# The order of work up to the first gate, written out anew, in a fused attention and expert kernel

## The chip, the cores and the metric

The kernel runs on one core of a Trainium2 chip. The metric is the device time of one execution in microseconds (us), lower is better. The profiler records one execution; all times inside it count from the start of its span.

## What is computed

```python
# attention with a decay, per batch (4), head (8); 576 tokens, 64 wide
scores = q @ k.T / 8 + (cum[:, None] - cum[None, :])    # cum = cumsum(log(clip(f, 1e-4, 1)))
attn = softmax(where(causal, scores, -1e9))
x = (attn @ v)            # heads side by side: (2304, 512)
# four experts, all used, weighted by p = domain_probs / sum
out = sum_e p[:, e] * (relu(x @ w1[e]) @ w2[e])          # w1: 512x1024, w2: 1024x512
```

## The kernel before

Attention is cut into jobs: a batch, a pair of heads and a part of the tokens (`half` 0: the first 256, `half` 1: the other 320). The output tokens are cut into nine chunks of 256. An expert's hidden units are cut into tiles of 128, and one weight tile holds the w1 columns (its columns 0 to 511) and the w2 rows (512 to 1023) of one such tile. A `Step` (L767) is one chunk against two weight tiles: `l1` gives the two tiles of hidden units, `gate` applies relu, `l2` multiplies by w2. Precision is kept by splitting an operand x into a rounded part (h) and the rest (l); a product is then three matmuls, h·h, h·l and l·h. A weight tile's rounded half (512 columns) is written by ScalarE (`w_hi`, L750), its rest by VectorE for even tiles of 2 to 14 and by GpSimd for the others (`w_lo`, L755). Even and odd tiles are the first and second of a step's two.

The work up to the first gate has an order of its own. The first four jobs (class `First`, L602; batch 0, first 256 tokens, two heads each, so heads 0 to 7) take plain fp32 products, all other jobs split ones. A head goes through: scores (`qk_pe`, L610), masked minimum (`qk_min`, L392, VectorE), exponential (`qk_exp`, L407, ScalarE), three transposes (`tr_pe`, L623), their copy out of PSUM (`tr_out`: ScalarE L634 for a pair's first head, VectorE L636 for its second), and the product with v (`av_pe`, L643). Per job, `recip` (L423, L426, L428: a tiny VectorE pair and a GpSimd copy) makes the reciprocal sums, `spread_out` transposes them (L451) and copies them out (L654, ScalarE), `scaled` multiplies (L658, VectorE, twice per job) and `fin` splits the result into `xh` and `xl`, on GpSimd (L669, L670) for jobs 0 to 2 and on ScalarE and VectorE (L672, L673) for job 3. After all four, step 0's `l1` can be finished; the hidden dimension of x is cut into four 128s, and block k comes from job k.

What sets the order: `startup` (L1083) runs in `tc.manual_schedule()`, so each engine keeps the order in which `startup` writes its instructions. Everything later is placed by a planner, which may also slip later instructions into a queue's gaps. `decays` (L143) makes the log decay rows: scans along the tokens (L115) of rows 0 and 1, and of all 32 rows, whose first 256 values then go by three small DMAs (L184) into row 64 of the other jobs' operands, so that one product adds scores and decay. `later_decays` (L193) scans the rest, splits it on ScalarE and VectorE (L197, L198), writes it to DRAM (L200), from where later jobs read it (L296), and issues the loads that follow, `w_load(3)` among them. All DMAs are issued from SP's queue. `W_HI` and `W_LO` (L33, L34) say after which head which half of weight tiles 0 to 3 is split.

Of the kernel before, what the change touches and what calls it, by code (L numbers as in the profile page):

```python
# [8 lines left out]
F32 = mybir.dt.float32  # L9
F32R = mybir.dt.float32r  # L10
AF = mybir.ActivationFunctionType
# [6 lines left out]
CH = 256  # L18
# [11 lines left out]
W_DVE = tuple(range(2, 16, 2))  # L30
LAST = (5, 6, 7, 8)
AHEAD = 10
W_HI = {2: ((0, 0),), 3: ((0, 512),), 4: ((1, 0),), 6: ((1, 512),), 7: ((2, 0), (2, 512)), 8: ((3, 0), (3, 512))}  # L33
W_LO = {**W_HI, 6: (), 7: ((1, 512),), 8: ((2, 0), (2, 512), (3, 0), (3, 512))}  # L34
JOBS = ((0, 0), (1, 0), (2, 0), (3, 0), (0, 1), (1, 1), (2, 1), (3, 1))


# [32 lines left out]
def fused(ctx: ExitStack, tc: tile.TileContext, qk, v, f, probs, w, out):  # L70
# [66 lines left out]
            )  # L137

    idle_ps = []
    wslot = {}  # L140
    vb = []

    def decays():  # L143
        for n in range(3, 9):
            x = xh_p.tile([128, NPR, CH], F32R, tag=("xl", "xh")[n % 2], name=f"wr{n}")
            wslot[n] = x.rearrange("p k n -> p (k n)").bitcast(F32)
        j = jobs[0]
        nc.sync.dma_start(out=row, in_=f[:2, :CH].rearrange("(o h) n -> o h n", o=1))
        nc.sync.dma_start(out=fr, in_=f)
        first_raw(0, (0,))  # L150
        first_raw(0, (1,))
        first_raw(1)
        first_raw(2)
        first_v(0)
        nc.vector.memset(ones, 1.0)
        nc.scalar.activation(out=warm, in_=ones[: B * H, :1], func=AF.Ln)
        nc.gpsimd.memset(jobs[0].kq[64:65, :, :CH], 8.0)
# [24 lines left out]
        scan(ncum[:, :CH], fr[:, :CH])  # L182
        for i in jobs[1:NPR]:
            nc.sync.dma_start(  # L184
                out=i.kq[64:65, :, CH:], in_=ncum[2 * i.pr : 2 * i.pr + 2, :CH]
            )
        first_raw(3)
        w_load(0)
        first_v(2)
        w_load(1)  # L190
        w_load(2)

    def later_decays():  # L193
        hi = xf_p.tile([128, 1024], F32R, tag="xf", name="nc_hi")[: B * H, :S]
        lo = scr2[: B * H, :S].bitcast(F32R)
        scan(ncum[:, CH:], fr[:, CH:], ncum[:, CH - 1 : CH])
        nc.scalar.activation(out=hi, in_=ncum, func=AF.Copy)  # L197
        nc.vector.tensor_tensor(out=lo, in0=ncum, in1=hi.bitcast(F32), op=ALU.subtract)  # L198
        for n, x in enumerate((hi, lo)):
            nc.sync.dma_start(out=ncd[:, n], in_=x.bitcast(F32))  # L200
        jobs[NPR].load()
        vb.append(acc_p.tile([128, 1024], F32, tag="acc", name="vb"))
# [30 lines left out]
            j.vs = slots[4][:, 256 * j.pr : 256 * j.pr + 256]  # L233

    def first_v(n):
        for j in jobs[n : n + 2]:
            nc.sync.dma_start(
                out=j.vs.rearrange("p (t h d) -> p t h d", t=2, h=2), in_=v[0, j.pr, :, :2]
            )

    def first_raw(n, heads_=(0, 1)):
        j = jobs[n]
# [359 lines left out]
    class First(Job):  # L602
# [24 lines left out]
                )  # L627
            self.tp[hh] = ps

        def tr_out(self, hh):  # L630
            n = 2 * self.pr + hh
            pt = self.pt[hh] = pt0[n % 2][:, 384 * (n // 2 % 3) : 384 * (n // 2 % 3) + 384]
            if hh == 0:
                nc.scalar.activation(out=pt, in_=self.tp[hh][:, :384], func=AF.Copy)  # L634
            else:
                nc.vector.tensor_copy(out=pt, in_=self.tp[hh][:, :384])  # L636

        def av_pe(self, hh):
            if hh == 0:
                self.o = ps_2.tile([128, 512], F32, tag="l2", name=f"o{self.nm}")  # L640
                self.xs = x_p.tile([128, 320], F32, tag="xs", name=f"xs{self.nm}")
            for jt, (a, z) in enumerate(((0, 256), (256, 384))):
# [10 lines left out]
            self.rc = x_p.tile([128, 320], F32, tag="tmp", name=f"rc{self.nm}")  # L653
            nc.scalar.activation(out=self.rc[:, :CH], in_=self.r[:, :CH], func=AF.Copy)  # L654

        def scaled(self, hh):
            a = slice(64 * hh, 64 * hh + 64)
            nc.vector.tensor_tensor(  # L658
                out=self.xs[a, :CH],
                in0=self.o[a, CH * hh : CH * hh + CH],  # L660
                in1=self.rc[a, :CH],
                op=ALU.mult,
            )

        def fin(self):
# [101 lines left out]
    class Step:  # L767
# [3 lines left out]
            self.nm = f"{s}_{g}_{c}_{ps}"  # L771

        def l1(self, q):
            if q == 0:
                self.l1p = ps_1.tile([128, 2, CH], F32, tag="l1", name=f"l1_{self.nm}")
            fi, kk = divmod(q, 2)
            th, tl = xh[self.c], xl[self.c]
            n = self.w0 + fi
            for k in (2 * kk, 2 * kk + 1):
                a = wh[n][:, k * 128 : (k + 1) * 128]  # L780
                z = wl[n][:, k * 128 : (k + 1) * 128]
                for m, (lhsT, rhs) in enumerate(((a, th), (a, tl), (z, th))):
                    nc.tensor.matmul(  # L783
                        out=self.l1p[:, fi, :],
                        lhsT=lhsT,
                        rhs=rhs[:, k, :],
                        start=(k == 0 and m == 0),
                        stop=(k == 3 and m == 2),
                    )

        def gate(self):
            self.gh = g_p.tile([128, 2, CH], F32R, tag="gh", name=f"gh{self.nm}")
            self.gl = g_p.tile([128, 2, CH], F32R, tag="gl", name=f"gl{self.nm}")
            nc.scalar.activation(out=self.gh, in_=self.l1p, func=AF.Relu)
            nc.vector.scalar_tensor_tensor(
                out=self.gl,
                in0=self.l1p,
                scalar=0.0,
                in1=self.gh.bitcast(F32),
                op0=ALU.max,  # L800
                op1=ALU.subtract,
            )

        def l2(self, q):
            tt, fi = divmod(q, 2)
# [276 lines left out]

    def startup():  # L1083

        def at(h):
            return heads[h] if 0 <= h < FIRST else (None, None)

        def scores(h):
            j, hh = at(h)
            if j:  # L1090
                j.begin(hh)
                j.qk_pe(hh, j.its)

        def mins(h):
            j, hh = at(h)
            if j:
                for t in j.its:
                    j.qk_min(hh, t)

        def exps(h):  # L1100
            j, hh = at(h)
            if j:
                for t in j.its:
                    j.qk_exp(hh, t)

        def close(j):
            for x in range(2):
                j.scaled(x)
            j.fin()

        first_slots()
        decays()
        scores(0)
        mins(0)
        exps(0)
        scores(1)
        mins(1)
        idle(256, 1)
        for s in range(FIRST + 1):
            (j, hh), (i, ii) = at(s), at(s - 1)  # L1120
            old = heads[s - 3][0] if s in (3, 5, 7) else None
            if s:
                scores(s + 2)
            if j:
                j.tr_pe(hh)
            if s == 0:
                scores(s + 2)
            exps(s + 1)
            if j:
                j.tr_out(hh)  # L1130
                if hh == 1:
                    j.recip()
            if s == FIRST:
                i.spread_out()
            if i:
                i.av_pe(ii)
            if old:
                old.spread_out()
            mins(s + 2)
            if old:  # L1140
                close(old)
            if s == FIRST:
                close(i)
            for n, a in W_HI.get(s, ()):
                w_hi(n, a, a + 512)
            for n, a in W_LO.get(s, ()):
                w_lo(n, a)
            if s == 1:
                later_decays()
# [113 lines left out]
```

## Time and profile before

| | |
|---|---|
| median of 3 runs | 977.52 us (975.76 to 978.43) |
| the profiled execution | 975.0 us, its span 973.2 us |
| TensorE busy in the span | 960.6 us, 99% |
| VectorE, ScalarE, GpSimd busy | 70%, 48%, 53% |
| granted TensorE clock, mean | 1.00 |
| bytes moved by DMA | 85.89 MB, 88 GB/s over the span |

The views are: the page's busy times; a table of stretches (windows); the chain of work that ended last, in order of time; and the timeline of one engine, where a row gives start, duration, engine, line, operation, output and inputs, and the count of instructions merged into it. In square brackets stands the idle time before the row, with what ended it.

### The profile page before, as it was taken

How to read it: one execution, taken by the hardware profiler on the slowest of the kernel's cores; microseconds unless marked ns; L12 is line 12 of the kernel's file. 1: busy time of each engine (PE TensorE's matmuls, PEld its weight loads, DVE VectorE, ACT ScalarE, POOL GpSimd, SP SyncE). 2: the span in 40 equal slices, each digit the busy share in tenths (PEclk: the TensorE clock that was granted, in tenths of full speed). 3: DMA queues.
4: the chain of work that ended last, by engine and by line, in shares of the span. 5: the costliest groups of instructions: out<-in, count | busy, mean ns of one | idle time of the engine just before them, and what ended most of it. 6: DMA issues, size and time to landing. Idle time of an engine off the chain costs nothing.

```text
span 973.2 us, 15567 instructions
## 1 busy us (share of the span) xinstructions
PE 960.6 (99%) x5638; PEld 843.7 (87%) x5638; DVE 676.4 (70%) x1413; ACT 467.2 (48%) x979; POOL 513.6 (53%) x511
## 2 busy tenths in 40 slices
PE   8999999999999999999999999999999999999998
PEld 6898999899899999998999998988788888888886
DVE  6877777877877676778769656357766666566665
ACT  7776664646656455556455544334323232233220
POOL 4988763502306547548457565778654444555410
PEclk9999999999999999999999999999999999999999
DMA  7765431322312312313313030421211112111002
GB/s 257 254 205 169 140 92 42 110 84 95 128 53 89 103 52 96 97 52 117 96 57 134 2 109 22 130 90 63 87 44 43 44 44 73 58 44 43 23 1 87
DMA packets 29822, 85.89 MB, mean 88 GB/s; under 512 B 3160, under 2 KB 5264, under 8 KB 29744
## 3 DMA queue, kind: packets, MB, share of 16 engines
q1 hardware_dynamic: 29744, 84.89, 26.8%
q8 instruction: 45, 0.74, 0.3%
q14 instruction: 33, 0.27, 0.1%
HBM read 80.00 MB, written 4.87 MB: 87 GB/s over the span
## 4 chain that ended last, share of the span: by engine, by line
PE 83%; POOL 5%; DVE 5%; issue 3%; DMA 2%; ACT 1%; SPq 0%; POOLq 0%; DVEq 0%; ACTq 0%
PE l L783 19%; PE l L813 19%; PE y L1011 17%; PE m L953 13%; PE s L378 5%; PE t L479 5%; PE o L529 5%; POOL bwl L933 2%; DMA wr<-in_w 2%; POOL wt L910 1%; POOL wl L755 1%; DVE v L313 1%; DVE kl L334 1%; POOL rx L895 1%; DVE rl L897 1%
## 5 line engine op out<-in xcount | busy, mean ns | idle before, releaser
L783 PE MATMUL l<-xl,wh 128*128 128x256 f32 x640 | 180.8, 283 | 0.3 <-DVE xl L673 0.3
L783 PE MATMUL l<-xh,wh 128*128 128x256 f32 x640 | 180.9, 283 | 0.2 <-ACT xh L672 0.2
L783 PE MATMUL l<-xh,wl 128*128 128x256 f32 x640 | 180.6, 283 | 0.0
L755 POOL TENSOR_TENSOR wl<-wr,wh 128x512 fp32r<-128x512 f32 x114 | 151.9, 1358 | 30.5 <-ACT wh L750 19.2
L835 DVE SCALAR_TENSOR_TENSOR acc<-y,prob,acc 128x512 f32<-128x512 f32 x120 | 88.3, 747 | 68.5 <-PE y L1011 68.5
L442 POOL TENSOR_SCALAR p<-p,rs 128x384 f32<-128x384 f32 (+2 forms) x72 | 107.8, 1513 | 50.1 <-DVE rs L438 46.8
L813 PE MATMUL l<-wh,gh 128*128 128x512 f32 x320 | 127.2, 397 | 0.8 <-DVE acc L835 0.8
L813 PE MATMUL l<-wl,gh 128*128 128x512 f32 x320 | 126.7, 396 | 0.0
L813 PE MATMUL l<-wh,gl 128*128 128x512 f32 x320 | 125.0, 394 | 0.0
L407 ACT ACTIVATE p<-p,nm 128x576 f32<-128x576 f32 (+2 forms) x160 | 95.6, 598 | 58.4 <-DVE nm L392 57.1
L783 PEld LDWEIGHTS l<-xl,wh 128*128 128x128 f32 x640 | 120.5, 188 | 3.3 <-DVE xl L673 0.5
L783 PEld LDWEIGHTS l<-xh,wh 128*128 128x128 f32 x640 | 120.4, 188 | 3.4 <-ACT xh L672 0.4
L933 POOL TENSOR_TENSOR bwl<-wr,bwh 128x256 fp32r<-128x256 f32 (+1 forms) x80 | 78.5, 1008 | 80.0 <-ACT bwh L930 80.0
L783 PEld LDWEIGHTS l<-xh,wl 128*128 128x128 f32 x640 | 120.4, 188 | 0.2
L392 DVE CUSTOM_DVE_ANT_0 p<-s,mask 128x288 f32<-128x288 f32 (+2 forms) x160 | 74.8, 478 | 57.6 <-PE s L378 52.4
L326 POOL CAST q<-raw 64x320 fp32r<-64x320 f32 (+1 forms) x56 | 27.3, 488 | 145.7 <-PE s L378 131.8
L1011 PE MATMUL y<-bwh,hh 128*128 128x512 f32 x256 | 101.2, 395 | 0.8 <-DVE acc L835 0.8
L1011 PE MATMUL y<-bwl,hh 128*128 128x512 f32 x256 | 101.1, 395 | 0.0
L1011 PE MATMUL y<-bwh,hl 128*128 128x512 f32 x256 | 100.4, 395 | 0.0
L953 PE MATMUL m<-rl,bwh 128*128 128x512 f32 x224 | 87.5, 390 | 0.0
L953 PE MATMUL m<-rh,bwh 128*128 128x512 f32 x224 | 87.4, 390 | 0.0
L953 PE MATMUL m<-rh,bwl 128*128 128x512 f32 x224 | 87.0, 392 | 0.0
(121 smaller groups left out, 2097.4 us busy)
## 6 DMA issues: line engine op xcount, KB each, us to landing
wr<-in_w SPq DMA_DIRECT2D x96, 512.0 KB
raw<-in_qk SPq DMA_DIRECT2D x16, 896.0 KB
raw<-in_qk SPq DMA_DIRECT2D x12, 512.0 KB
vr<-in_v SPq DMA_DIRECT2D x16, 320.0 KB
out<-acc SPq DMA_DIRECT2D x16, 256.0 KB
vr<-in_v SPq DMA_DIRECT2D x8, 128.0 KB
first<-in_qk SPq DMA_DIRECT2D x3, 256.0 KB
first<-in_v SPq DMA_DIRECT2D x4, 128.0 KB
```

The lines of the kernel that those rows point to most:

```text
L378: nc.tensor.matmul(out=ps[:, at : at + z - a], lhsT=lhsT, rhs=rhs, start=(m == 0), stop=(m == 1),)
L392: nc.vector.tensor_tensor_reduce(out=pt[:, a:z], in0=ps, in1=mask[:, m0 + a : m0 + z], scale=-0.125, scalar=BIG if n == 0 else nm[:, col : ...
L407: return nc.scalar.activation(out=pt[:, :w_], in_=pt[:, :w_], func=AF.Exp, scale=-1.0, bias=self.nmax[hh][:, c : c + 1], accum_out=self.ss ...
L442: eng.tensor_scalar(out=x, in0=x, scalar1=rs[:, i : i + 1], scalar2=None, op0=ALU.mult)
L479: nc.tensor.transpose(ps[:, at : at + 128], self.p[hh, it][:, TOK0[jt] : TOK0[jt] + 128], ident)
L755: eng.tensor_tensor(out=wl[n][:, a:z], in0=wraw[n][:, a:z], in1=wh[n][:, a:z].bitcast(F32), op=ALU.subtract)
L783: nc.tensor.matmul(out=self.l1p[:, fi, :], lhsT=lhsT, rhs=rhs[:, k, :], start=(k == 0 and m == 0), stop=(k == 3 and m == 2),)
L813: nc.tensor.matmul(out=l2[tt], lhsT=lhsT, rhs=rhs, start=(self.ps == 0 and fi == 0 and m == 0), stop=(self.ps == 1 and fi == 1 and m == 2),)
L835: nc.vector.scalar_tensor_tensor(out=acc[c][:, tt, :], in0=ps, scalar=sc, in1=acc[c][:, tt, :], op0=ALU.mult, op1=ALU.add,)
L933: nc.gpsimd.tensor_tensor(out=lo[:, a:z], in0=x[:, a:z], in1=hi[:, a:z].bitcast(F32), op=ALU.subtract)
L953: nc.tensor.matmul(out=ps, lhsT=lhsT[:, o], rhs=rhs[:, k, :], start=(k == 0 and i == 0), stop=(k == 1 and i == 2),)
L1011: nc.tensor.matmul(out=ps, lhsT=lhsT, rhs=rhs, start=(fi == 0 and m == 0), stop=(fi == 1 and m == 2),)
```

## The change

Six edits, all before or in step 0. (1) `decays`: clamps and logs go first for all three inputs, then the scans, the 32-row one second; only job 0's v is loaded ahead of the decay rows, job 1's after them; w tile 0 comes before job 3's q and k; two of GpSimd's row fills go to VectorE. (2) `later_decays` is cut in two: the scan of the rest stands right after head 0's transposes, its split is on GpSimd; the DMAs follow after head 2's minimum. (3) A head's product with v takes only that head's 64 columns of v, so that the two heads of a job fill 64 partitions each of the same 256 columns, and `scaled` is one VectorE operation. (4) `startup` is written out line by line. (5) Step 0's first products go pair by pair: block k of both weight tiles, then block k+1, in two PSUM tiles, with two gates of half the width. (6) Of the weight tiles 0 to 3, the w1 halves are split first, the w2 halves later.

```diff
@@ decays
         first_raw(1)
+        first_v(0)
         first_raw(2)
-        first_v(0)
...
-        for i in jobs[1:NPR]:
-            nc.gpsimd.memset(i.kq[64:65, :, :CH], 8.0)
+        for i, eng in zip(jobs[1:NPR], (nc.vector, nc.vector, nc.gpsimd)):
+            eng.memset(i.kq[64:65, :, :CH], 8.0)
...
-        for h in range(2):
-            clamp(row[:, h])
-            log(row[:, h])
+        rows = (row[:, 0], row[:, 1], fr)
+        for x in rows:
+            clamp(x)
+        for x in rows:
+            log(x)
+        nc.scalar.activation(out=warm, in_=ones[: B * H, :1], func=AF.Exp)
         scan(j.kq[64:65, 0, CH:], row[:, 0])
-        clamp(fr)
-        log(fr)
-        nc.scalar.activation(out=warm, in_=ones[: B * H, :1], func=AF.Exp)
+        scan(ncum[:, :CH], fr[:, :CH])
         scan(j.kq[64:65, 1, CH:], row[:, 1])
-        scan(ncum[:, :CH], fr[:, :CH])
         for i in jobs[1:NPR]:
             nc.sync.dma_start(
                 out=i.kq[64:65, :, CH:], in_=ncum[2 * i.pr : 2 * i.pr + 2, :CH]
             )
+        first_v(1)
+        w_load(0)
         first_raw(3)
-        w_load(0)
         first_v(2)
+        first_v(3)
         w_load(1)
         w_load(2)
-    def later_decays():
+    def far_decays():
...
-        nc.scalar.activation(out=hi, in_=ncum, func=AF.Copy)
-        nc.vector.tensor_tensor(out=lo, in0=ncum, in1=hi.bitcast(F32), op=ALU.subtract)
-        for n, x in enumerate((hi, lo)):
+        nc.gpsimd.tensor_copy(out=hi, in_=ncum)
+        nc.gpsimd.tensor_tensor(out=lo, in0=ncum, in1=hi.bitcast(F32), op=ALU.subtract)
+        ncs.extend((hi, lo))
+    def later_decays():
+        for n, x in enumerate(ncs):
             nc.sync.dma_start(out=ncd[:, n], in_=x.bitcast(F32))
...
@@ First.tr_out, av_pe, scaled
-            if hh == 0:
+            if on_scalar:
...
+            c = slice(64 * hh, 64 * hh + 64)
-                    out=self.o[:, CH * hh + TOK0[jt] : CH * hh + CH],
-                    lhsT=self.vr[:, jt],
+                    out=self.o[c, TOK0[jt] : CH],
+                    lhsT=self.vs[:, 128 * jt + 64 * hh : 128 * jt + 64 * hh + 64],
...
-        def scaled(self, hh):
+        def scaled(self):
             nc.vector.tensor_tensor(
+                out=self.xs[:, :CH], in0=self.o[:, :CH], in1=self.rc[:, :CH], op=ALU.mult
             )
@@ startup, the new order
         scores(0)
+        idle(256, 1)
+        scores(1)
         mins(0)
         exps(0)
         mins(1)
         idle(256, 1)
+        turn(0)
+        far_decays()
+        exps(1)
+        scores(2)
+        turned(0)
+        scores(3)
+        mins(2)
+        later_decays()
+        turn(1)
+        exps(2)
+        jobs[0].recip()
+        av(0)
+        mins(3)
+        turned(1)
+        scores(4)
+        turn(2)
+        exps(3)
+        w_hi(0, 0, 512)
+        av(1)
+        mins(4)
+        turned(2)
+        w_lo(0, 0)
+        scores(5)
+        turn(3)
+        exps(4)
+        jobs[0].spread_out()
+        jobs[1].recip()
+        av(2)
+        mins(5)
+        close(0)
+        turned(3)
+        scores(6)
+        w_hi(1, 0, 512)
+        turn(4)
+        exps(5)
+        av(3)
+        jobs[1].spread_out()
+        mins(6)
+        turned(4)
+        w_lo(1, 0)
+        scores(7)
+        turn(5)
+        exps(6)
+        mins(7)
+        exps(7)
+        jobs[2].recip()
+        av(4)
+        turned(5)
+        close(1)
+        turn(6)
+        turned(6)
+        av(5)
+        jobs[3].recip()
+        jobs[2].spread_out()
+        turn(7)
+        turned(7)
+        close(2)
+        av(6)
+        jobs[3].spread_out()
+        w_hi(0, 512, 1024)
+        av(7)
+        w_hi(1, 512, 1024)
+        w_hi(2, 0, 512)
+        l1(0)
+        l1(1)
+        w_lo(0, 512)
+        close(3)
+        w_lo(1, 512)
+        w_hi(3, 0, 512)
+        w_lo(2, 0)
+        w_lo(3, 0)
+        l1(2)
+        l1(3)
         j = heads[FIRST][0]
         j.prep_v_hi()
+        w_hi(2, 512, 1024)
         j.prep(0)
-        for q in range(4):
-            steps[0].l1(q)
         steps[0].gate()
+        w_hi(3, 512, 1024)
+        w_lo(2, 512)
+        w_lo(3, 512)
         j.prep_v_lo()
```

## Rows read from the trace of the kernel before

**Rows 1.** The page: busy us, share of the span and instructions of each engine.

```profile
PE 960.6 (99%) x5638; PEld 843.7 (87%) x5638; DVE 676.4 (70%) x1413; ACT 467.2 (48%) x979; POOL 513.6 (53%) x511
```

**Rows 2.** Windows: us, busy us and count by engine, granted clock, DMA share, GB/s.

```profile
20.00:25.00 5.00, 3.80 (x23) 2.74 (x22) 3.53 (x12) 4.09 (x13) 4.41 (x7) 1.00 1.01 351
...
27.50:32.00 4.50, 4.50 (x37) 4.49 (x38) 4.47 (x5) 4.23 (x10) 4.50 (x4) 1.00 1.02 410
32.00:40.00 8.00, 8.00 (x50) 7.12 (x49) 7.04 (x15) 4.77 (x10) 7.55 (x10) 1.00 0.87 338
```

**Rows 3.** The chain that ended last, 25 to 35 us: start, us, what.

```profile
25.49 0.42 DVE xs L658
...
25.92 0.44 DVE xs L658
...
26.38 0.43 ACT xh L672
...
26.83 0.62 DVE xl L673
...
27.49 4.47 PE l L783 x36
31.96 2.74 PE l L813 x12
```

**Rows 4.** Timeline of TensorE: scores of heads 2 and 3; step 2's first l·h product.

```profile
9.16 1.55 PE L610 MATMUL s<-first 65*128 65x128 f32 x8 [0.76 <-issue]
...
35.25 0.28 PE L783 MATMUL l<-xh,wl 128*128 128x256 f32 x1
```

**Rows 5.** Timeline of SP's queue.

```profile
4.49 1.06 SPq L237 DMA_DIRECT2D first<-in_v  x2
6.25 1.92 SPq L184 DMA_DIRECT2D first<-ncum  x3
...
20.27 0.53 SPq L296 DMA_DIRECT2D kl<-ncd  x2
```

**Rows 6.** Timeline of VectorE.

```profile
12.37 0.87 DVE L115 TENSOR_TENSOR_SCAN ncum<-scr,ncum 32x320 f32<-32x320 f32 x1
13.99 0.75 DVE L198 TENSOR_TENSOR scr<-ncum,nc_hi 32x576 fp32r<-32x576 f32 x1 [0.75 <-ACT nc_hi L197]
...
15.83 1.27 DVE L423 TENSOR_SCALAR ss<-ss 128x4 f32<-128x4 f32 x1
...
27.36 2.40 DVE L755 TENSOR_TENSOR wl<-wr,wh 128x512 fp32r<-128x512 f32 x2
...
33.19 1.39 DVE L755 TENSOR_TENSOR wl<-wr,wh 128x512 fp32r<-128x512 f32 x2
```

**Rows 7.** Timeline of ScalarE.

```profile
13.27 0.68 ACT L197 ACTIVATE nc_hi<-ncum 32x576 fp32r<-32x576 f32 x1 [1.86 <-DVE ncum L115]
13.86 0.39 ACT L407 ACTIVATE p<-p,nm 128x128 f32<-128x128 f32 x1
...
14.74 0.46 ACT L634 ACTIVATE pth_first<-t 128x384 f32<-128x384 f32 x1
15.11 0.61 ACT L750 ACTIVATE wh<-wr 128x512 fp32r<-128x512 f32 x1
...
23.62 1.15 ACT L750 ACTIVATE wh<-wr 128x512 fp32r<-128x512 f32 x2
```

**Rows 8.** Timeline of GpSimd.

```profile
15.80 1.27 POOL L755 TENSOR_TENSOR wl<-wr,wh 128x512 fp32r<-128x512 f32 x1 [3.33 <-ACT wh L750]
...
18.68 0.40 POOL L669 CAST xh<-xs 128x256 fp32r<-128x256 f32 x1 [0.91 <-DVE xs L658]
19.16 0.73 POOL L670 TENSOR_TENSOR xl<-xs,xh 128x256 fp32r<-128x256 f32 x1
...
25.88 1.28 POOL L755 TENSOR_TENSOR wl<-wr,wh 128x512 fp32r<-128x512 f32 x1
27.39 3.52 POOL L755 TENSOR_TENSOR wl<-wr,wh 128x512 fp32r<-128x512 f32 x2 [0.24 <-ACT wh L750]
```

More of the change, by code (lines that the diff above doesn't have):

```diff
@@ L139, in fused @@
     idle_ps = []
+    ncs = []
     wslot = {}
@@ L152, in decays @@
         first_raw(1)
+        first_v(0)
         first_raw(2)
[L154 removed]
         nc.vector.memset(ones, 1.0)
         nc.scalar.activation(out=warm, in_=ones[: B * H, :1], func=AF.Ln)
[L157 removed]
+        nc.gpsimd.memset(j.kq[64:65, :, :CH], 8.0)
         nc.gpsimd.memset(mask, 0.0)
@@ L235, in first_v @@
     def first_v(n):
[L236 to L239, printed above, removed]
+        j = jobs[n]
+        nc.sync.dma_start(
+            out=j.vs.rearrange("p (t h d) -> p t h d", t=2, h=2), in_=v[0, j.pr, :, :2]
+        )
     def first_raw(n, heads_=(0, 1)):
@@ L773, in l1, with l1_part @@
         def l1(self, q):
-            if q == 0:
-                self.l1p = ps_1.tile([128, 2, CH], F32, tag="l1", name=f"l1_{self.nm}")
             fi, kk = divmod(q, 2)
+            for k in (2 * kk, 2 * kk + 1):
+                self.l1_part(fi, k)
+        def l1_part(self, fi, k, apart=False):
+            if fi == k == 0:
+                x = ps_1.tile([128, 2, CH], F32, tag="l1", name=f"l1_{self.nm}")
+                self.l1p = [x] if not apart else [x[:, :1, :]]
+            elif apart and k == 0:
+                x = ps_2.tile([128, 512], F32, tag="l2", name=f"l1_{self.nm}")
+                self.l1p.append(x.rearrange("p (h n) -> p h n", h=2)[:, :1, :])
             th, tl = xh[self.c], xl[self.c]
             n = self.w0 + fi
[L779 to L789, printed above, removed]
+            a = wh[n][:, k * 128 : (k + 1) * 128]
+            z = wl[n][:, k * 128 : (k + 1) * 128]
+            for m, (lhsT, rhs) in enumerate(((a, th), (a, tl), (z, th))):
+                nc.tensor.matmul(
+                    out=self.l1p[fi][:, 0, :] if len(self.l1p) > 1 or apart else self.l1p[0][:, fi, :],
+                    lhsT=lhsT,
+                    rhs=rhs[:, k, :],
+                    start=(k == 0 and m == 0),
+                    stop=(k == 3 and m == 2),
+                )
         def gate(self):
@@ L793, in gate @@
             self.gl = g_p.tile([128, 2, CH], F32R, tag="gl", name=f"gl{self.nm}")
[L794 to L802, printed above, removed]
+            at = 0
+            for ps in self.l1p:
+                gh, gl = (x[:, at : at + ps.shape[1], :] for x in (self.gh, self.gl))
+                at += ps.shape[1]
+                nc.scalar.activation(out=gh, in_=ps, func=AF.Relu)
+                nc.vector.scalar_tensor_tensor(
+                    out=gl,
+                    in0=ps,
+                    scalar=0.0,
+                    in1=gh.bitcast(F32),
+                    op0=ALU.max,
+                    op1=ALU.subtract,
+                )
         def l2(self, q):
@@ L1083, in startup, with turn, turned, av @@
     def startup():
-        def at(h):
-            return heads[h] if 0 <= h < FIRST else (None, None)
+        H_ = heads[:FIRST]
         def scores(h):
[L1089 to L1092, printed above, removed]
+            j, hh = H_[h]
+            j.begin(hh)
+            j.qk_pe(hh, j.its)
         def mins(h):
[L1095 to L1098, printed above, removed]
+            j, hh = H_[h]
+            for t in j.its:
+                j.qk_min(hh, t)
         def exps(h):
[L1101 to L1109, printed above, removed]
+            j, hh = H_[h]
+            for t in j.its:
+                j.qk_exp(hh, t)
+        def turn(h):
+            H_[h][0].tr_pe(H_[h][1])
+        def turned(h):
+            H_[h][0].tr_out(H_[h][1], h % 2 == 0 or h == 7)
+        def av(h):
+            H_[h][0].av_pe(H_[h][1])
+        def close(n):
+            jobs[n].scaled()
+            jobs[n].fin()
+        def l1(k):
+            for fi in range(2):
+                steps[0].l1_part(fi, k, True)
         first_slots()
@@ L1113, in startup @@
         scores(0)
+        idle(256, 1)
+        scores(1)
         mins(0)
         exps(0)
-        scores(1)
         mins(1)
         idle(256, 1)
[L1119 to L1149, printed above, removed]
+        turn(0)
```

9 lines of the change are left out of this document (1 added, 8 removed).

## Prediction

> **What bounds the kernel now.** The page's busy times come first: TensorE is busy 960.6 of 973.2 us [rows 1], so an edit elsewhere counts only by how much sooner, or later, TensorE gets into its unbroken run. The table of stretches shows where that is: 3.80 of 5 us busy from 20 to 25, all of 4.50 and of 8.00 from 27.5 to 40 [rows 2]. In the same two stretches VectorE (4.47, 7.04) and GpSimd (4.50, 7.55) are full too, and the DMA share is 1.02 and 0.87 [rows 2]: whatever comes sooner on TensorE soon asks them for weight halves sooner. The chain in order of time tells what ends last at the start: `scaled` of job 3 in two pieces from 25.49, then `xh` from 26.38, `xl` from 26.83, and 27.49, when TensorE can go on [rows 3]. From there 36 first products of 0.12 us, then step 0's second products at about 31.9 [rows 3]; the last is the landmark I count to, with step 2's first l·h product at 35.25 [rows 4] behind it.
>
> **Two things the rows show that set prices.** First, VectorE and GpSimd hold each other up when both read two operands from SBUF: `recip`'s tiny operation of 128x4 at 15.83 took 1.27 us, to 17.10, while a GpSimd split ran from 15.80 to 17.07 [rows 6, 8]; and from 27.4 on two VectorE halves took 2.40 us and two GpSimd halves 3.52, which adds up as strict turns of about 0.6 and 1.2 us [rows 6, 8]. The Trainium skill says so too (SBUF — State Buffer): the shared port pair is held by one of the two for a whole instruction and not split; by that, and by the trace, each VectorE split can wait for one GpSimd split. I take turns, whoever waited longer going first. Second, ScalarE's split of the far decays at 13.27 waited 1.86 us for the scan [rows 7], head 3's exponentials behind it started only at 13.86 [rows 7], and VectorE's part at 13.99 waited 0.75 more [rows 6].
>
> **The change part by part.** I follow the new order engine by engine with the durations of the rows. The old order followed the same way gives the end of job 3's `xl` at 27.42; the chain has 27.45 [rows 3].
>
> *Start, fewer transfers.* Scores of head 2 wait 0.76 us, to 9.16 [rows 4], for the decay rows issued from 6.25 [rows 5]. The two v loads that SP issued at 4.49 [rows 5] are now one ahead and one behind, and the 32-row scan is second of three instead of last (about 0.6 us sooner): scores of head 2 near 8.5. Bounds: nothing (9.1) to 0.7. It costs nothing and gives nothing at the end, because of the next step. The row fills put on VectorE lie in its wait for the first input, and clamping all three inputs ahead delays scan 0 by about 0.6 us, with exponential 0 waiting for its table load either way: nothing.
>
> *Far decays.* The scan (0.87) [rows 6] now runs at 7.7 to 8.5, in VectorE's gap. GpSimd's copy and subtraction of 32x576 are not in the trace: by length from 128x256 (0.40 and 0.73) and 128x512 (1.28) [rows 8] about 0.9 and 1.45, so 8.6 to 10.9; bounds 1.1 us (as 128x256) and 3.3 (twice the rate). ScalarE loses 0.68, VectorE 0.75. `recip` of job 0 is then ready at 10.1, but waits for the port to 10.85; minimum 3 comes at 11.1, exponentials of head 3 at 11.4 instead of 13.86 [rows 7]: 2.4 us sooner.
>
> *ScalarE's order to head 7.* From 11.4: four heads' exponentials of 0.88 (13.86 to 14.74), two copies of 0.37 (14.74 to 15.11) [rows 7], two reciprocals of 0.28, two halves of 0.55 (1.15 for two) [rows 7], and about 1.1 us of waits for spread transposes, the longer one at 16.2 to 17.0, where head 3's product waits for its copy, behind `scaled` on VectorE. Sum 7.0 to 7.2: head 7's exponentials at 18.6 to 19.55. `recip` of job 3 then waits for GpSimd's `xl` of job 1 (0.73) [rows 8], the reciprocal copy is out at 21.0, the last product with v starts at 21.3.
>
> *Half-wide products, one `scaled`.* The moving columns are the same, so the product costs the same. `scaled` of job 3 falls from 0.42 and 0.44 to one [rows 3]: done at 22.7 instead of 26.36, 3.65 sooner.
>
> *Three weight halves ahead of `xh`.* On ScalarE the w2 halves of tiles 0 and 1 and the w1 half of tile 2 stand between the last reciprocal (21.6 to 22.0) and `xh`: three of 0.55, so `xh` runs at 23.5 to 23.9, giving back 0.8 us. GpSimd's two splits of those w2 halves run at 22.5 to 25.05, and `xl` waits for the port: its end is 25.43, against 27.45, 2.0 sooner.
>
> *Pair by pair.* After `xl` stand 5 of step 0's products instead of 13: 8 x 0.12 = 0.95 us sooner, so step 1 begins at 26.1, 2.95 sooner. The two gates of half the width cost one more instruction each on ScalarE and VectorE, hidden behind step 1's 2.8 us of products; if that cover went, about 0.3 each (half of the 0.61 of a 128x512 operation [rows 7]).
>
> *What is late next.* In the turns of the port, GpSimd's half of tile 3 has waited longer than VectorE's half of tile 2 and goes first: tile 2's rest is ready at 27.2, and step 1's third product, due at 26.3, waits 0.9. Step 0's second products then start 2.0 sooner. VectorE's turns go on (second half of tile 2, four small splits of v, tile 4, each behind a GpSimd piece): tile 4's rest is ready at about 34.1, where before it was at 33.9 (half of the 1.39 from 33.19) [rows 6]. The old order followed the same way gives 34.4, 0.5 too late, so 33.6 here: step 2's l·h product is 1.6 sooner than 35.25 [rows 4]. Tile 3's load is no bound: the reads ahead of it in SP's queue waited till 20.27 for the decays' write [rows 5], which is now done some 3 us sooner.
>
> **Sum.** 2.4 + 1.25 (ScalarE's order and `scaled`) - 0.8 (halves ahead) - 0.85 (`xl` at the port) + 0.95 (pairs) - 0.95 (tile 2's rest) = 2.0 sooner at step 0's second products; 1.6 to 2.0 after tile 4. I take 1.9. The profiled execution's 975.0 becomes 973.1. The median shown, 977.52, is 2.5 above that execution; to it the forecast is 975.6.
>
> **Rivals.**
> - *The port falls well* (chance 0.34). If VectorE's half of tile 2 goes ahead of GpSimd's half of tile 3, or the planner puts other products in the gap, the whole 2.95 stays: 974.6; if `xl` too finds the port free, another 1.0: 973.5. For it: at 27.36 VectorE went first [rows 6, 8]. Against: there GpSimd's operand was not yet written, here it is since 24.4.
> - *The half-wide products cost more* (chance 0.12). The trace has no such product. A matmul's record is 0.28 long against a spacing of 0.12 [rows 3, 4]; if the pipe had to empty at each change of width, 0.16 at two changes for each of eight products is 2.6 us, of which the walk leaves 1.4 on the path: 977.0. The Trainium skill has this rule (TensorEngine Tiling (Array Packing), Key Properties: changing the mode drains TensorE); whether a 64-column operand counts as another mode no row here shows. The least is a gain of nothing, since the moving columns set the time.
> - *Slower: tile 4 too late* (chance 0.07). Between `xl` and tile 4's rest VectorE takes the port eight times. If each waits a full GpSimd split, 8 x 1.28 + 3.4 of its own is 13.6, from 25.4 to 39.0 instead of 33.9, and step 2 would stand 3.8 later than before: up to 981.3; if only GpSimd's seven ready pieces come between (6.9 us, and 0.9 for the gates), 36.2, and 978.5. It decides once tile 4's rest comes after 35.25. For it: VectorE and GpSimd are full there [rows 2]. Against: GpSimd has not so many pieces ready.
>
> **How the numbers follow.** My forecast has chance 0.47. A measurement of this kernel tells about 0.3%, 2.9 us, from no change. The forecast's gain of 1.9 lies inside; the well-falling port's 2.95 to 4.0 mostly beyond, and with the scatter of the runs shown (2.7 us) some of my own case too: faster 0.33. Slower by more needs the upper half of the last rival: 0.03. The rest, 0.64, is within 0.3%. The range takes 973.5 with some scatter on one side and 977.0 with some on the other: 973.0 to 977.9.
>
> **What would show it.** Head 3's exponentials near 11.4; `recip` of job 0 about 0.8 us long beside GpSimd's 32x576 subtraction; job 3's `xl` ending at 25.4 and long beside a GpSimd split; step 1's l·h product waiting for VectorE's tile 2; step 0's second products near 29.8; after 40 us the same work as before, shifted. I am wrong if tile 2 goes first at the port, if the half-wide products of a head take TensorE longer than the full ones did, or if TensorE shows new gaps after 35 us.

## The result: 987.34 us, about 10 us slower, and the profile after

The changed kernel takes 987.34 us (median of 4 runs, 984.22 to 988.96) beside 977.42 of the kernel before: a ratio of 1.0101, interval 1.0079 to 1.0122. Forecast were 975.6 us, range 973.0 to 977.9. The profiled execution took 988.9 us.

The page's busy times after (span 987.1), which answer to [rows 1]:

```profile
PE 975.9 (99%) x5640; PEld 852.4 (86%) x5640; DVE 675.5 (68%) x1410; ACT 467.3 (47%) x980; POOL 514.2 (52%) x511
```

TensorE is busy 15.3 us longer with nearly the same work (5640 records beside 5638); its idle time is 11.2 us, before it was 12.6. So the loss is no wait in the first place: the same products take longer. The table of stretches (columns as in [rows 2]) shows where:

```profile
20.00:25.00 5.00, 5.00 (x18) 3.33 (x17) 1.53 (x6) 2.15 (x8) 0.87 (x2) 1.00 0.96 333
```

From 20 to 25 us TensorE is never idle (3.80 of 5 us before), yet VectorE is down from 3.53 to 1.53 us there and GpSimd from 4.41 to 0.87: everyone waits for TensorE. Its timeline gives the reason (in brackets the idle time ahead of a row):

```profile
5.37 1.62 PE L614 MATMUL s<-first 65*128 65x128 f32 x4 [0.34 <-DVE first L113]
...
11.72 2.93 PE L614 MATMUL s<-first 65*128 65x128 f32 x8 [1.11 <-DMA first<-ncum]
14.44 0.85 PE L627 MATMUL t<-ident,p 128*128 128x128 f32 x3
15.22 1.54 PE L648 MATMUL o<-pth_first,first 128*64 128x256 f32 x4
...
34.28 0.49 PE L627 MATMUL t<-ident,p 128*128 128x128 f32 x3
```

The scores of heads 2 and 3 (eight records: a plain fp32 product stands as two, and "head 2's eight products" below counts these records, while idle products are counted whole) take 2.93 us where the kernel before took 1.55 [rows 4], and three transposes 0.85 where from 34 us on they take 0.49. Spacings of nearly double length are the lower of TensorE's two levels, 1.2 against 2.4 GHz (with eight idle products, below, the same 2.93 stands beside a granted clock of 0.50). They last from 5.37 to 33 us, so in this execution the level was low before TensorE waited for head 2's rows. The column of the granted clock says 1.00 all the while, so here the level has to be read from the spacing. (The Trainium skill warns of that in TensorE: Matmul & The Clock Gate, Seeing it yourself: recorded clock events have been seen to be unreliable. This trace agrees: 1.00 beside doubled spacings.)

Second, head 2's scores come at 11.72 instead of 9.16. The chain that ended last names what they wait for, and SP's queue shows why it is late:

```profile
6.37 5.31 DMA first<-ncum
11.68 0.04 issue
11.72 2.93 PE s L614 x8
```

```profile
4.47 0.54 SPq L248 DMA_DIRECT2D first<-in_qk  x1
5.05 0.60 SPq L290 DMA_DIRECT2D vr<-in_v  x1
5.69 0.56 SPq L281 DMA_DIRECT2D raw<-in_qk  x1
6.37 1.91 SPq L183 DMA_DIRECT2D first<-ncum  x3
```

Two loads that the diff doesn't mention, v (128 KB) and q and k (896 KB) of a later job, now stand ahead of the decay rows. In the kernel before the planner had put the same two behind weight tile 2, issued at 11.39 and 11.87. It may fill gaps in SP's queue, and here it did. With 1.05 MB ahead of them the rows land 5.3 us after their issue.

### The profile page after: what moved, and what is told of

The parts are those of the page before. It is cut to its first block, busy times and chain, and to the rows that moved or that the text cites. A ratio compares the mean times of both kernels' runs of the same rounds, so it can differ in the third digit from the quotient of the medians.

```text
span 987.1 us, 15571 instructions
## 1 busy us (share of the span) xinstructions
PE 975.9 (99%) x5640; PEld 852.4 (86%) x5640; DVE 675.5 (68%) x1410; ACT 467.3 (47%) x980; POOL 514.2 (52%) x511
## 4 chain that ended last, share of the span: by engine, by line
PE 84%; POOL 5%; DVE 5%; issue 3%; DMA 2%; ACT 2%; POOLq 0%; ACTq 0%; DVEq 0%
PE l L791 19%; PE l L825 19%; PE y L1023 16%; PE m L965 12%; PE s L382 5%; PE t L483 5%; PE o L533 5%; POOL bwl L945 2%; DMA wr<-in_w 1%; POOL wt L922 1%; POOL wl L756 1%; PE o L648 1%; PE s L614 1%; DVE v L317 1%; DVE kl L338 1%
## 5 line engine op out<-in xcount | busy, mean ns | idle before, releaser
L330 POOL CAST q<-raw 64x320 fp32r<-64x320 f32 (+1 forms) x56 | 27.1, 483 | 145.8 <-PE s L382 134.8
```

## The experiments

The kernel before was timed again beside each group: 977.28 us (23 runs) beside e1 to e4, 977.22 (30) beside e5 to e8, 977.04 (35) beside e9 to e12, 976.86 (21) beside e13 and e14; each ratio is to those runs. Three theories stood at first: (A) the 0.34 us gap ahead of head 0's scores keeps TensorE at the lower level; (B) the half-wide products do; (C) the wait for the late rows.

**Three theories, four kernels.** Two single edits of the changed kernel, one that puts the rows first (the later jobs' loads are tied to a point in SP's queue behind weight tile 2), and both together:

```diff
# e1_idle8
-        idle(256, 4)
+        idle(256, 8)
# e2_full_width
-                    out=self.o[c, TOK0[jt] : CH],
-                    lhsT=self.vs[:, 128 * jt + 64 * hh : 128 * jt + 64 * hh + 64],
+                    out=self.o[:, CH * hh + TOK0[jt] : CH * hh + CH],
+                    lhsT=self.vr[:, jt],
...
# e3_rows_first, in decays and in the planner's step
         w_load(2)
+        sp_mark.append([i for i in nc.cur_bb.bb.instructions if i.engine == mybir.EngineType.SP][-1])
...
-            with behind() if at < stage_end[FIRST] else ExitStack():
+            with behind() if at < stage_end[FIRST] else ExitStack(), tc.issue_after(sp_mark[0]):
                 asteps[at][1]()
# e4_idle8_rows: e1 and e3
```

> The changed kernel with 8 idle products instead of 4 ahead of head 0's scores, so that TensorE has no gap between them. In the profile after, every product up to 33 us stands twice as far apart as before (head 0's scores 1.62 us for 0.8), and TensorE idled 0.34 us ahead of them. Theory A, the gap early in the run leaves TensorE at the lower of its two levels (1.2 GHz): spacing of the products falls to that of before by 6 us at the latest, step 1 begins near 29, 976 to 979 us. Theory B, the half-wide products keep it low: still doubled up to 30 us or later, 985 to 990. Theory C, the wait for the decay rows up to 11.7 us, behind two loads of 1.05 MB that the planner slipped ahead of them, keeps it low: still doubled, 985 to 990.

Measured: 983.52 us, ratio 1.0068 (1.0042 to 1.0093).

> The changed kernel with a head's product with v on all 128 columns of v, and scaled in two pieces, as before. Theory A (early gap): head 0's scores still 1.6 us apart, 984 to 990. Theory B (half-wide products): the spacing falls to that of before soon after the first product with v (15 us), 977 to 981. Theory C (wait for the rows): 984 to 990.

Measured: 981.99 us, ratio 1.0055 (1.0035 to 1.0075).

> The changed kernel with the later jobs' loads held behind w tile 2 in SP's queue, so that the 128 KB and 896 KB loads no longer stand ahead of the decay rows. All theories: head 2's scores begin at 8 to 9.5 us instead of 11.72. Theory A (early gap): the products still stand twice as far apart up to about 30 us, 983 to 987. Theory B: the same, 983 to 987. Theory C: without the wait of 1.1 us the level rises by about 10 us, 975 to 979.

Measured: 975.87 us, ratio 0.9986 (0.9972 to 1.0000).

> Both edits: 8 idle products and the later loads behind w tile 2. Theory A: full rate by 6 us and rows by 9.5, so what was forecast for the change itself, 973 to 977, job 3's xl ending near 25.5 and waiting for the port beside a GpSimd split. Theory B: doubled spacing up to about 30 us, 983 to 987. Theory C: as theory A, 973 to 977.

Measured: 975.44 us, ratio 0.9985 (0.9972 to 0.9997).

Holding the later jobs' loads back alone takes 11.5 us off, more than the loss. Without the early gap 6 us of the loss are left, with full width 5. With the rows in time TensorE starts from the same low level as in the changed kernel, but without the wait it is at the full rate by head 2:

```profile
7.63 1.49 PE L616 MATMUL s<-first 65*128 65x128 f32 x4
...
10.28 1.48 PE L616 MATMUL s<-first 65*128 65x128 f32 x8
```

The timeline of TensorE with eight idle products shows what the late rows do. It is at full rate, waits 3.36 us, and is at the lower level when the wait ends and until 25.5; its table of stretches has the granted clock of that:

```profile
6.65 0.82 PE L614 MATMUL s<-first 65*128 65x128 f32 x4
...
12.80 2.93 PE L614 MATMUL s<-first 65*128 65x128 f32 x8 [3.36 <-DMA first<-ncum]
...
16.30 1.54 PE L648 MATMUL o<-pth_first,first 128*64 128x256 f32 x4
...
25.57 0.92 PE L614 MATMUL s<-first 65*128 65x128 f32 x4
```

```profile
6.60:9.40 2.80, 2.80 (x16) 2.15 (x15) 1.45 (x9) 1.44 (x7) 0.00 (x0) 1.00 1.01 250
12.80:15.50 2.70, 2.70 (x8) 2.26 (x9) 0.90 (x6) 0.67 (x3) 0.01 (x1) 0.50 1.07 219
15.50:24.00 8.50, 8.50 (x28) 5.58 (x26) 2.75 (x15) 3.18 (x12) 2.05 (x3) 0.50 0.85 281
```

With full-width products (and four idle ones) the wait is longer, 3.75 us, but the full rate is back at 17.9:

```profile
11.96 2.93 PE L614 MATMUL s<-first 65*128 65x128 f32 x8 [3.75 <-DMA first<-ncum]
...
16.61 1.49 PE L614 MATMUL s<-first 65*128 65x128 f32 x4
17.89 0.54 PE L627 MATMUL t<-ident,p 128*128 128x128 f32 x3
```

**Is it the wait, or the level behind it, and does the kernel before suffer too?**

```diff
# e5_before_bytes_first, the kernel before
+        w_load(0)
+        w_load(1)
         for i in jobs[1:NPR]:
             nc.sync.dma_start(
                 out=i.kq[64:65, :, CH:], in_=ncum[2 * i.pr : 2 * i.pr + 2, :CH]
             )
         first_raw(3)
-        w_load(0)
         first_v(2)
-        w_load(1)
         w_load(2)
# e6_filled_wait: e1 and, in startup
         exps(1)
+        idle(256, 8)
         scores(2)
```

> The kernel before, with the loads of weight tiles 0 and 1 (two of 524 KB) ahead of the three decay rows in SP's queue, nothing else changed: full-width products with v, the old order of startup. Theory C (the bytes ahead of the rows are the cause, and need nothing else of the change): scores of head 2 wait about 2.5 to 3.5 us and come at 11.5 to 12.5, TensorE's products are at the spacing of the lower level after the wait (2.9 for head 2's and 3's eight instead of 1.55), and the time is 980 to 983, as with the full-width products in the changed kernel (981.99). Rival (only together with the new order do the bytes cost anything, the old order has slack for them): 977 to 978.5.

Measured: 982.33 us, ratio 1.0053 (1.0034 to 1.0073). Theory C holds with nothing else of the change. The rows need 7.5 us from their issue (6.64) to head 2's scores, more than forecast, as two whole weight tiles stand ahead of them:

```profile
7.95 1.09 PE L623 MATMUL t<-ident,p 128*128 128x128 f32 x3 [0.63 <-ACT p L407]
14.16 2.90 PE L610 MATMUL s<-first 65*128 65x128 f32 x8 [5.12 <-issue]
```

The wait for the rows did not bring the level down here: the granted clock is 0.53 from 8 to 9 us already, behind waits of 0.27 and 0.63 only, and stays low until 21.7. And the larger part of this loss is the wait itself: head 2's scores are 5.0 us later than before, while the way behind them is 2.8 longer (91.18 against 88.34, table below).

> The changed kernel with eight idle products instead of four at the start, and eight more (about 0.43 us each) in the place where TensorE waits 3.36 us for the decay rows; the rows themselves come as late as before the edit. Theory that the level is the price (TensorE's idle time ahead of head 2's scores brings the lower level, and that costs most): head 2's scores at 12.8 to 13.2, eight products at the spacing of the full rate (1.5 instead of 2.93), all after it as with the rows first but 2.5 to 2.8 later, time 978.0 to 979.0. Rival (the late rows themselves cost it, through the chain behind them): as without the filling, 983.5.

Measured: 978.60 us, ratio 1.0014 (1.0002 to 1.0026). Head 2's scores are later still, but TensorE doesn't idle ahead of them, and 4.9 of the 983.52 are gone:

```profile
9.94 3.62 PE L133 MATMUL idle<-scr 128*128 128x256 f32 x16
13.40 1.48 PE L614 MATMUL s<-first 65*128 65x128 f32 x8
```

So in this kernel about 3 us of the late rows' price are the wait itself (978.60 against 975.44 with rows in time), and the larger part is the lower level that follows when TensorE idles through it.

**The width again, and the kernel before's own waits.**

```diff
# e9_idle8_full: e1 and e2 together
# e12_before_filled, the kernel before
         mins(1)
-        idle(256, 1)
+        idle(256, 2)
...
             if s == 0:
+                idle(256, 1)
                 scores(s + 2)
```

> The changed kernel with eight idle products at the start (as in the run that took 983.52) and full-width products with v besides; the decay rows stay late. It differs from that run in the width alone. Theory B (half-wide products lengthen the stretch at the lower level): head 2's scores as late as there (12.5 to 13), eight products at the lower spacing (2.9), but the full rate is back by 20 instead of 25.5; the product after the 0.92 us wait that all runs have near 100 us (107.19 there, 98.65 with the rows first) comes at 103 to 104, and the time is 979.5 to 981.5. Rival (how long the lower level lasts has nothing to do with the width): 983 to 984, and 106.5 to 107.5 for that product.

Measured: 980.41 us, ratio 1.0031 (1.0018 to 1.0044): 3.1 less than with half-wide products. In the profiled execution the wait was 1.68 us only, head 2's eight products took 1.69, and the lower level lasted from about 13.0 to 16.4:

```profile
11.71 1.69 PE L614 MATMUL s<-first 65*128 65x128 f32 x8 [1.68 <-DMA first<-ncum]
```

The forecasts that head 2's scores would come at 12.5 to 13, and be at the lower spacing already, 2.9, missed. B holds as an amplifier: the level comes down about the wait, and with half-wide products it stays down longer. These two profiles differ in the wait too (1.68 and 3.36), but full width with four idle products has the longer wait, 3.75, and 6 us of the lower level where half width has 13 behind 3.36. The medians say the same (987.34 to 981.99 with four idle products). Why the width does that is not shown.

> The kernel before with two more idle products, one after head 1's minimum and one ahead of head 2's scores, where its TensorE waits 0.64 and 0.76 us. No other work changes, and neither product is as long as its wait. Theory (the lower level after a wait of TensorE also hits the kernel before, in a part of its executions: about half of them take 978.3 to 980.6 with a mean granted clock of 0.994 to 0.998, the others 974.9 to 977.4): most of those above 978 vanish, median 975.3 to 976.3. Rival (the waits ahead of head 2 have nothing to do with that): 977.2, the same two groups.

Measured: 975.52 us, ratio 0.9985 (0.9975 to 0.9996). Of the 35 executions of the kernel before beside it, 8 have a mean granted clock of 0.994 or 0.995 and take 977.8 to 980.3; with the waits filled none of 12 is under 0.997 or over 976.91. Two idle products of TensorE, and no other work, give 1.5 us of the 1.9 that the whole change was forecast to give. Where the clock falls in those 8 executions no profile shows; the bytes-first kernel, whose TensorE works in the same order up to 8 us, has such a fall behind waits of 0.27 and 0.63. And the 8 explain a part only: the other 27 have a median of 976.36.

**What the new order gives with the rows in time.** Five edits on the rows-first kernel, and half-wide products alone in the filled kernel before:

```diff
# e7_rows_full: e3 and e2. e8_port_order: e3 and, in startup
         exps(6)
+        w_hi(0, 512, 1024)
+        w_hi(1, 512, 1024)
+        w_lo(0, 512)
...
-        w_hi(0, 512, 1024)
         av(7)
-        w_hi(1, 512, 1024)
         w_hi(2, 0, 512)
         l1(0)
         l1(1)
-        w_lo(0, 512)
-        close(3)
-        w_lo(1, 512)
+        jobs[3].scaled()
+        w_lo(2, 0)
+        jobs[3].fin()
         w_hi(3, 0, 512)
-        w_lo(2, 0)
         w_lo(3, 0)
+        w_lo(1, 512)
# e10_scan0_first: e8, clamps and logs of rows[0] and rows[2], scan 0, then rows[1]
# e11_not_paired: e8 without l1(0) to l1(3), and after the last w_lo
+        for fi in range(2):
+            for k in range(4):
+                steps[0].l1_part(fi, k, True)
# e13_port_full: e8 and e2. e14_before_half: e12 with the change's av_pe and scaled
```

> The rows-first kernel with the products with v and the multiplication by the reciprocal as they were before (full width, two multiplications). The half-wide products stand at 0.80 per head at the full rate in the rows-first kernel, the full-width ones at 0.66 in the kernel before. Theory that half-wide products cost 0.14 each and that about half of the eight lie on the path: 0.4 to 0.6 sooner by the products, 0.43 later by the second multiplication: 975.6 to 976.1, no difference that shows in the time; the spacing shows in the profile (a head's two products in 0.66). Rival (the half-wide products cost nothing): 976.3.

Measured: 977.52 us, ratio 0.9999 (0.9982 to 1.0015); a head's two products at 0.65, as expected. The time missed both forecasts and is 1.65 us over rows first: 10 of the 12 executions have a mean granted clock of 0.998 or less (rows first: 3 of 10), and in the profiled one it falls near 98 us (last section).

> The rows-first kernel with another order at the end of startup: ScalarE writes the w2 halves of tiles 0 and 1 in its gap before head 7's exponentials, GpSimd's rest of tile 0's w2 half follows at once, tile 2's rest on VectorE goes ahead of job 3's xh and xl, GpSimd's tile 3 and tile 1's w2 half come after them. Theory that the port's turns at 25 to 30 us cost the path what the trace shows (xl 0.44 late, tile 2's rest 0.84 late, xh 0.5 behind three weight halves): xl ends at 27.1 instead of 28.25, step 1 has no wait at its third product, step 0's second products at 30.6 to 31.0 instead of 32.84, time 973.8 to 974.6. Rival (what is late next takes it back: tile 4's rest or the next weight half on the port binds after 33 us anyway): 975.4 to 975.9.

Measured: 975.10 us, ratio 0.9977 (0.9965 to 0.9990), the lowest median of all, but between the two ranges. Its timeline of TensorE has head 2's scores where the forecast had them (8.5), step 0's second products 1.43 sooner than before (31.80; forecast 30.6 to 31.0), `xl` ending at 26.37 (forecast 27.1), and a new wait behind:

```profile
8.53 1.55 PE L616 MATMUL s<-first 65*128 65x128 f32 x8
...
30.37 0.39 PE L827 MATMUL l<-wh,gh 128*128 128x512 f32 x1
...
44.76 0.50 PE L827 MATMUL l<-wh,gl 128*128 128x512 f32 x1 [0.78 <-DVE gl L809]
...
97.13 0.39 PE L535 MATMUL o<-pth,v 128*128 128x256 f32 x1 [0.92 <-ACT pth L495]
```

> The kernel with rows first and the port's order mended (975.10), with head 0's clamp, log and scan ahead of the clamp of head 1's row, so that TensorE's wait between its idle products and head 0's scores (0.66 there, 0.34 with rows first) goes. Theory A (that wait costs time in some executions, by the lower level): head 0's scores at 4.7 to 4.9 without a wait, products at the spacing of the full rate from about 6 at the latest, median 974.4 to 974.9 and no execution above 976.5. Rival (the order of scans makes no difference to the end): 975.1, with executions up to 977.5 as there.

Measured: 976.20 us, ratio 0.9988 (0.9977 to 1.0000); head 0's scores at 4.83 without a wait, but slowest 977.54: theory A, a miss.

> The kernel with rows first and the port's order mended (975.10), with step 0's first products tile by tile again: 24 in a row behind job 3's xh and xl instead of half of them ahead of it. Theory of the prediction (after job 3's xl stand 13 of step 0's first products instead of 5: 8 x 0.12 = 0.95 us): step 0's second products 0.9 later than 30.37 for the same start, time 975.8 to 976.2. Rival (other waits take it up, the weight rests first): 975.0 to 975.3.

Measured: 976.34 us, ratio 0.9993 (0.9975 to 1.0011). Its step 0's second products start at 30.10, 0.27 sooner than with pairs, head 2's scores at the same time (8.54): the pairs give nothing once `xl` is in time. The median's difference from 975.10 is no support for them either, as the fastest executions are level (974.59 and 974.73).

> The kernel with rows first and the port's order mended (975.10), with full-width products with v and two multiplications. Theory (the half-wide products take the gain back, 8 x 0.14 = 1.1 us of TensorE, of which the second multiplication returns 0.43): TensorE busy about 960.5 instead of 961.6, the product after the 0.92 us wait near 97 us comes 0.3 to 0.7 sooner than 97.13 for the same start of head 2's scores, the fastest executions at 974.1 to 974.4 instead of 974.7. Rival (a later wait of TensorE takes it back whatever the start does): the same product at 96.9 to 97.4, the fastest executions at 974.7, and the wait of 0.5 to 0.8 near 44 us stays or grows.

Measured: 976.26 us, ratio 0.9999 (0.9986 to 1.0011), fastest 974.67, as the rival had it; its landmark (97.9 for the same start) and its wait near 44 us (0.39, at 45.22) missed. The 0.14 us per head return as waits, one of them for VectorE's rest of a weight tile (timeline of TensorE):

```profile
22.56 0.44 PE L457 MATMUL b<-ident,rb 128*128 128x128 f32 x2 [1.12 <-POOL rb L434]
...
34.77 0.39 PE L794 MATMUL l<-xh,wl 128*128 128x256 f32 x1 [0.55 <-DVE wl L759]
```

> The kernel before with its two waits filled (975.52, fastest 974.57), with half-wide products with v and one multiplication, the old order otherwise. Theory (a head's product is 0.14 longer at the full rate, and one multiplication of 0.43 goes): a head's two products at 0.80 instead of 0.66 in the profile, head 2's scores to the product near 97 us 0.2 to 0.7 longer than 88.39, median 975.7 to 976.2. Rival (the half-wide products' extra length lies in waits of TensorE in the old order, and the multiplication is a gain): 975.0 to 975.3, that distance 0.2 to 0.4 shorter.

Measured: 977.10 us, ratio 0.9998 (0.9989 to 1.0007), fastest 975.25. A head's two products are at 0.80 apart from the next work, as expected, and the way to the product near 97 us is 88.69, 0.30 longer than 88.39, as expected. The median is 1.6 over the filled kernel's 975.52, more than expected, but the two stand beside different runs of the kernel before and their ratios' intervals overlap. So in the old order half-wide products cost some 0.3 us of TensorE's way; a loss in the time is not shown, nor is one in the new order with the rows in time.

**One view over all runs.** Near 97 us every kernel has the same product behind the same 0.92 us wait (for `pth`). Its start less that of head 2's scores, in the profiled executions, is free of how late the rows were:

| kernel | head 2's scores | the product | difference | median |
|---|---|---|---|---|
| before | 9.16 | 97.50 | 88.34 | 977.04 to 977.52 |
| after | 11.72 | 110.35 | 98.63 | 987.34 |
| eight idle products | 12.80 | 107.19 | 94.39 | 983.52 |
| the same, wait filled | 13.40 | 101.83 | 88.43 | 978.60 |
| the same, full width, not filled | 11.71 | 100.85 | 89.14 | 980.41 |
| full width, four idle products | 11.96 | 102.40 | 90.44 | 981.99 |
| before, bytes first | 14.16 | 105.34 | 91.18 | 982.33 |
| rows first | 10.28 | 98.65 | 88.37 | 975.87 |
| rows first, eight idle products | 10.38 | 98.64 | 88.26 | 975.44 |
| rows first, port order | 8.53 | 97.13 | 88.60 | 975.10 |
| before, waits filled | 8.78 | 97.17 | 88.39 | 975.52 |

Of the runs left out, the difference is 88.07 in rows first at full width, 88.57 with scan 0 first, 88.32 without pairs, 88.69 in the filled kernel before at half width, and 89.37 in the port order's kernel at full width, whose waits stand above. So where the rate is full behind head 2, old order or new, the way to that product is 88.1 to 88.7 us. All that goes beyond, 10.3 us in the changed kernel, is the lower level; the wait for the rows adds 2.56 (11.72 less 9.16). Together 12.85 of the profiled execution's 13.9 us. Behind the product near 97 us the granted clock falls in some executions (0.69 from 110 to 115 us in the changed kernel); that is in the times, not in these differences. (Head 2's scores are at 10.28 in rows first because the products of heads 0 and 1 are at the lower spacing in that execution, 1.62 and 1.49 us for four; with the same start they are at 0.89 and 0.92 in that of the port order.)

## Why the prediction was wrong

*Start, fewer transfers* failed first. It read the diff's order of the startup's own transfers and took the rest of SP's queue as it was in [rows 5]. The planner's part of that queue came out another way for the changed kernel, and 1.05 MB slipped ahead of the rows. Head 2's scores came at 11.72, where the forecast had 8.5; with rows first and the port's order they came at 8.53. The sentence "costs nothing and gives nothing at the end" priced this step from one side only. A bound above ("the rows come behind a later load") would have had a row: the kernel before already waits 0.76 there [rows 4].

*No rival had the lower level.* The profiled execution of the kernel before shows no sign of it, and the forecast costed a wait at its own length. Measured with eight idle products, the late rows (3.36 us of waiting) cost about 8 (983.52 against 975.44), of which the filled wait gave back 4.9.

*Half-wide products, "the product costs the same"*: wrong by 0.14 a head at the full rate (0.80 against 0.66) and about 0.2 at the lower level (1.48 against 1.28), and they keep the lower level longer. The 0.80 and 0.66 are the ways from one start to the next (rows first, then the kernel before):

```profile
12.01 0.86 PE L650 MATMUL o<-pth_first,first 128*64 128x256 f32 x4
12.81 0.92 PE L616 MATMUL s<-first 65*128 65x128 f32 x4
```

```profile
10.88 0.82 PE L643 MATMUL o<-pth_first,first 128*128 128x256 f32 x4
11.54 0.82 PE L610 MATMUL s<-first 65*128 65x128 f32 x4
```

The rival that priced them had the sign right and, at 0.32 a head, twice the size. By the Trainium skill, TensorEngine Tiling (Array Packing), Key Properties, a change of mode drains TensorE. The spacing would agree in sign, but whether a change of width is one was not tried.

*Far decays* was about right: 0.65 and 1.40 us on GpSimd (forecast 0.9 and 1.45), `recip` of job 0 held up to 1.35 us beside it in the port order's kernel (forecast 0.8), head 3's exponentials there at 11.86 (forecast 11.4). (The prediction's "both read two operands" is more than its row says: `recip`'s operation reads one tensor.)

*Three weight halves ahead of `xh`* and *What is late next* were right in kind. In the changed kernel the chain has them as forecast, only some 14 us later (`xh` at 37.91, forecast 23.5), and TensorE waits 0.44 us for `xl` (forecast to end 0.85 late) and 0.84 for tile 2's rest (forecast 0.9):

```profile
36.35 1.56 ACT wh L751 x3
37.91 0.31 ACT xh L673
...
39.70 1.78 DVE wl L756
```

*Pair by pair*, 0.95 sooner: not found. Without the pairs the second products came no later (30.10 against 30.37). *Tile 4 too late* was not found either: in the changed kernel TensorE has no wait between 41.53 and the one near 110 us. (The sum of that rival's second bound, 25.4, 3.4, 6.9 and 0.9, is 36.6 and not 36.2.)

*The sum* of 1.9 us is not in any run. It walked ScalarE's order, 2.4 and 1.25 us sooner, and in rows first TensorE itself binds: it has no wait from head 2's scores to 27.8. From these scores to step 0's second products the kernel before takes 22.64 us, 2.24 of them waits; rows first takes 22.40, with 1.28 of waits, and the forecast had 21.3. The longer half-wide products (8 x 0.14 = 1.1) take back the most of what the waits gave; at full width the waits are 2.24 again and it takes 22.20.

Rows first has a median of 975.87, the forecast 975.6, but that agreement is not the forecast's merit: its way behind head 2 is 88.37 us, that of the kernel before 88.34, and the fastest executions are 974.21 and 974.91. The medians differ in part, as its filled version suggests, because some of the kernel before's executions lose their rate at its own waits ahead of head 2. Where step 0's second products do come 1.43 sooner, in the port order's kernel, 0.37 is left at 97 us: 0.78 goes into the wait at 44.76. What takes the rest isn't settled: without half-wide products the gain did not come back.

## What to carry to other kernels

Read the whole queue of the changed build, not the diff: a planner may answer a change in one place with a large transfer ahead of a small, urgent one. Pin such transfers behind a mark when a small transfer is on the path. Price a wait of TensorE by what its rate is afterwards; where a wait can't be avoided, cheap products that fill it (two here, 975.52) can be worth about as much as a new order of the work (975.10).

## What the runs showed of the hardware that was not expected

Behind waits of 1.68 us (full width), 3.75 (full width) and 3.36 (half width) ahead of head 2 TensorE was at the lower level for about 3, 6 and 13 us. The fall does not stand at the wait's end: behind 1.68 it came 1.3 us later (granted clock 1.00 from 12 to 13 us, 0.52 from 13 to 14), with 3.36 it came within the wait, and with bytes first ahead of it, behind waits of 0.27 and 0.63. Other waits of 0.40 to 1.12 at the full rate, before 30 us, were not followed by a fall (1.05 at 24.25 in the kernel before, 1.12 at 22.56 above). The 0.92 us wait near 97 us goes either way: the granted clock falls behind it in 8 of the 16 profiled executions. With rows first and full width the granted clock falls behind it, in the kernel before it doesn't (tables of stretches of the former, then of the latter):

```profile
98.00:100.00 2.00, 1.85 (x9) 1.64 (x10) 2.00 (x11) 1.79 (x7) 1.40 (x4) 0.73 0.23 66
100.00:102.00 2.00, 2.00 (x10) 2.00 (x11) 1.93 (x8) 1.03 (x5) 1.50 (x2) 0.50 0.40 51
102.00:104.00 2.00, 2.00 (x18) 2.00 (x17) 0.69 (x3) 0.60 (x1) 0.00 (x0) 0.91 0.55 212
```

```profile
98.00:100.00 2.00, 1.94 (x15) 1.78 (x15) 2.00 (x9) 1.84 (x6) 1.57 (x3) 1.00 0.24 67
100.00:102.00 2.00, 2.00 (x20) 2.00 (x19) 1.93 (x8) 1.07 (x3) 0.93 (x2) 1.00 0.73 196
```

Six microseconds at a mean of 0.71 lose 1.7 us, nearly the whole forecast of 1.9, at a wait that no edit here touched. The medians of the kernels with the rows in time (975.10 to 977.52) lie within 2.4 us, little more than one such fall, so they hardly rank these kernels. What decides whether the clock falls there is open.
